# Gated attention beside an MLP on one core: a fourth up product early, PV output in two PSUM banks, x pieces on ScalarE's queue

## The chip, the core and the metric

The kernel runs on one of the eight cores of a Trainium2 chip. A core has five engines with an instruction stream each: TensorE (PE, matrix products into PSUM), VectorE (DVE), ScalarE (ACT), GpSimd (POOL) and SyncE (SP, which here only issues DMAs). The metric is the device time of one execution in microseconds (us), the median of several runs.

## The reference

All arrays are float32; x has 2048 rows of 640.

```python
xn = layernorm(x)                              # no scale, eps 1e-5
q = xn @ wq                                    # 32 heads of 128
k, v = the last 512 rows of the caches         # per head, no mask
p = softmax(q @ k.T * 128**-0.5)
s = (p @ v over all heads) @ wo                # 2048 x 640
h = relu(xn @ w1 + b1) ** 2                    # 640 -> 1728
g = silu(h @ w2 + b2)                          # 1728 -> 640
out = x + s * g
```

## The kernel before, in words

**Number format.** Every product is made of three float32r matmuls: each operand is split into a rounded high part and the remainder, and high x high, high x low and low x high are added in PSUM (`triple`, `products`). A "triple" of three 128x128x512 matmuls is the unit of PE's work; every split costs a copy (ACT) and a subtraction (DVE or POOL).

**Stages.** The 2048 rows are four tiles of 512 columns (the work is done transposed: features on partitions, rows along the free axis).

1. For tiles 0 to 2 the MLP: 14 chunks f of the hidden width, an up product (15 matmuls) and a down product (15 matmuls) each; the gate g goes to DRAM (`g_d`). Meanwhile the normalised x of each tile is written to DRAM in its two parts (`xT_d`).
2. Attention in 128 units: two halves of the rows, sixteen groups of two heads, two tiles, two heads. A unit has scores s (12 matmuls into four PSUM banks), the query product pq of two units later (15), the PV product o (12) and, for a pair of units, the output projection r (30).
3. The MLP of tile 3 (`late_*` functions): its up and down products (`lu`, `ly`) fill the last units and the tail after them, and the last gate, product with s and store end the kernel.

**A unit's softmax.** DVE folds each score bank to maxima (`max_fold`, tile rdm), ACT gathers 32-partition pieces (`gather`), DVE reduces them to a row (rowm); SP writes the row to DRAM (`m_d`) and loads it back spread over all partitions (`bm`), DVE subtracts it (`shift`, writes e and so frees the score banks), ACT takes the exponential (`expo`), ACT and POOL split it (`p_hi`, `p_lo`, tile pt). POOL adds the two halves (su), DVE folds the sum (`s_fold`, rds), ACT gathers, DVE inverts (sq, rows), SP writes and spreads it (`s_d`, `bs`), and DVE scales the PV output (`o_norm`), which ACT and DVE split (ot).

**Order.** From stage 2 on, the order is written out by hand: `at` and `on` put each step into `plan` with a due time, a unit's length being taken as PERIOD = 12.4 us, and at the end the steps are recorded in the order of these times. Every engine works strictly in its order, SP's queue too: a DMA that waits holds those behind it. The due times only sort; what an engine really waits for are semaphores.

**What the change touches.** `early_up`: three of tile 3's fourteen up products (chunks 11 to 13) are made during units 0 to 3, when there is no r and no early o to fill PE; their relu, square and split go to SBUF, and both parts to DRAM (`h_d`), from where `late_h` loads them in the tail. `q_mm` for unit 1 stands before unit 0. `load_xT` for the second half loads twenty pieces of 256 KB (two tiles, five column groups, two parts) on SP in units 59 to 64, in pairs at two places of a unit. `v_mm` writes every unit's o into one bank (tag "o"); r and pq use the banks "qr0" and "qr1"; `psx` is one more bank, used by early products and at the end. `finish` multiplies the first half's s by g and adds x in ten units of the second half.

In the tail, SP's order in unit 127 is: l1r3 (weights), five loads of x for the last gate (`late_x`, lx), then the unit's m_d and bm, later s_d and bs, and after these the weight loads l1r5 and l1r6. l1r6's buffer is free when POOL has split l1r4.

Of the kernel before, what the change touches and what calls it, by code (L numbers as in the profile page):

```python
# [8 lines left out]
F32 = mybir.dt.float32  # L9
# [11 lines left out]
def kernel(  # L21
# [65 lines left out]
    h_d = {f: dpool.tile([P, 2, NT], F32, name=f"h_d{f}") for f in range(FC - 3, FC)}  # L87

    def raw(ap):
        return ap.bitcast(F32)  # L90
# [19 lines left out]

    w1s, w2s = [], []
    for f, (f0, n) in enumerate(chunks):
        wp = wpa if f < FA else wpb
        if n < P:
            w1s.append([wp.tile([P, DC, 2 * n], F32R, name=f"w1s{f}")])
        else:
            if f < FA - 1:
# [312 lines left out]
    NQ = NT // B32  # L430
    NH = KC // 2

    EN = {"d": dve, "p": pool}

    XT, ACC, KT, VV, WQ, WO, Q, E, SC, MB, RD, PT, PO, OT, RB, QPS, FX, CL, PRS, RAW = (
        {} for _ in range(20)
    )
# [16 lines left out]
            for i in range(2)  # L454
        ]

    def load_xT(hf, t, i, cs):
        sp.dma_start(raw(XT[hf, t][i])[:, cs, :], xT_d[hf * TPH + t][i][:, cs, :])

    def raw_tile(kind, name):  # L460
        n = D if kind in "qo" else W
# [25 lines left out]
    def q_mm(i, cs):  # L487
        hf, g, t, h = units[i]
        if 0 in cs:
            QPS[i] = bank(f"pq{i}", int(i != 1))  # L490
# [150 lines left out]
    def load_finish(n, hf, t, d):  # L641
# [8 lines left out]
            }[n],  # L650
        )

    def finish(hf, t, d):
        fx, fg = (FX.pop((n, hf, t, d)) for n in "xg")
        a = ACC[hf, t][:, d, :] if hf else FX.pop(("s", hf, t, d))
        em, ea = "dp" if hf == 0 else "dd"
        EN[em].tensor_tensor(a, a, fg, op=ALU.mult)
        EN[ea].tensor_tensor(a, a, fx, op=ALU.add)
        store(sp, hf, t, d, a)

    def store(q, hf, t, d, a):
# [74 lines left out]
            c == DC - 1,  # L736
        )

    def early_split(f):
        r = LR.pop(f)  # L740
        hi, lo = (
            ap.tile([P, NT], F32R, tag=f"raw{n}", name=f"eh{f}_{n}", bufs=1) for n in "xg"
        )
        act.activation(hi, r, AF.Copy)
        dve.tensor_tensor(lo, r, raw(hi), op=ALU.subtract)
        for k, h in enumerate((hi, lo)):
            sp.dma_start(h_d[f][:, k, :], raw(h))

    def late_h(f):
        kind, bufs = ("wv", G) if f < FC - 1 else ("q", AHEAD + 1)  # L750
        LH[f] = pair(kind, [P, NT], f"lh{f}", bufs)
        for k in range(2):
            sp.dma_start(raw(LH[f][k]), h_d[f][:, k, :])

    def late_relu(f, kind):
        n = chunks[f][1]
        ph = LPH.pop(f)
# [9 lines left out]
    def late_square(f, eng=pool):  # L767
        eng.tensor_tensor(LR[f], LR[f], LR[f], op=ALU.mult)

    def late_split(f):  # L770
        n = chunks[f][1]
# [40 lines left out]
        store(sp, HALF - 1, TPH - 1, d, a)  # L812

    steps_n = len(steps)
    opened = (LATE - 1) * FC + FA
    for n in range(steps_n):
        mlp_step(n)
        if n == opened:
# [62 lines left out]
    for t in range(TPH):  # L881
        for c in range(DC):
            k, late = divmod(c + 1 - t, 2)
            w = (NG * UPG + t * G - 3 - AHEAD + t + k) * PERIOD + (8.5 if late else -1.6)
            if c == 0:
                at(w, open_xT, 1, t)
            for i in range(2):
                at(w + 0.7 * i, load_xT, 1, t, i, slice(c, c + 1))
    R_AT = (
        ((2 * PERIOD + 11.25, range(G)),),  # L890
        ((3 * PERIOD + 2.75, range(G)),),
# [9 lines left out]
    for i in range(NU):  # L901
        t0 = i * PERIOD

        def on(when, f, *a):
            at(t0 + when, f, *a)

        hf, g, t, h = units[i]
        for c in range(KC):
            on(0.68 * c, s_mm, i, c)
        if i + AHEAD < NU:  # L910
            q_at = 3.45 if i % G and i > UPG else 4.3
            for c in range(DC):
                on(q_at + 0.68 * c, q_mm, i + AHEAD, (c,))
            on(q_at + 3.5, q_hi, i + AHEAD)
            on(q_at + 4.1, q_lo, i + AHEAD)
# [12 lines left out]
        on(PERIOD + 6.2, s_fold, i)  # L928
        on(PERIOD + 8.0, gather, i, "s")
        on(PERIOD + 8.5, row, i, "s")  # L930
        on(18.6, p_lo, i, 1)
        for c in range(KC):
            on(PERIOD + 8.5 + 0.68 * c, v_mm, i, c)
        on(2 * PERIOD + 4.2, o_norm, i)
        on(2 * PERIOD + 4.9, o_hi, i)
        on(2 * PERIOD + 5.5, o_lo, i)
        if i % G == G - 1:
            for d in range(DC):
                last = i == NU - G - 1
# [19 lines left out]
    for item in order:  # L959
# [8 lines left out]
            at(now + 1.36, r_acc, NU - 1, n)  # L968
        else:
            for k, d in enumerate(range(DC)):  # L970
                for f in range(FC - 3, FC):
                    DOWN_AT.setdefault(f, now)
                    at(now + 0.68 * (3 * k + f - FC + 3), late_down, f, (d,))
                at(now + 2.04 * (k + 1), late_gate, d)
        now += STEP[kind]
    PREP = {
        0: z - 2 * PERIOD + 8.4,
# [31 lines left out]
    for f, u in sorted(DOWN_AT.items()):  # L1009
        free = DOWN_AT[f - 4] + STEP["d"] + 0.2 if f > 3 else 0.0  # L1010
        PREP2[f] = max(free, u - 7.0) if f else u - 5.0
        at(PREP2[f - 2] + 0.9 if f > 1 else u - 12.0, late_load, 2, f)
        at(PREP2[f], late_prep, 2, f)
        if f >= FA:
            at(now - 8.0 - 4.0 * (FC - f), late_h, f)
    EARLY_IN = (0,) * 7 + (1,) * 3 + (2,) * 3 + (3,) * 2
    for n, u in enumerate(EARLY_IN):
        k, c = divmod(n, DC)
        f = FA + k
        at(u * PERIOD + 8.0 + 0.01 * n, early_up, f, k % 2, c)  # L1020
        if c == DC - 1:
            at(u * PERIOD + 10.6, late_relu, f, "s")
            at(u * PERIOD + 12.0, late_square, f, dve)
            at((u + 1) * PERIOD + 7.6, early_split, f)
    at(z + 2.0, late_x)
    for d in range(DC):
        for n in "xg":
            at(z + 30.0 + 8.0 * d, load_finish, n, HALF - 1, 0, d)
        at(z + 36.0 + 8.0 * d, finish, HALF - 1, 0, d)
    for when, k, f, a in sorted(plan, key=lambda e: e[:2]):  # L1030
        f(*a)
# [46 lines left out]
```

## Time and profile before

| | |
|---|---|
| runs | 1979.72, 1978.24, 1979.13 us; median 1979.13 |
| profiled execution | 1978.84 us, its span 1977.1 us |
| mean granted TensorE clock | 0.999 |
| PE busy | 1952.0 us, 8576 matmuls |
| chain that ended last | PE 87%, DVE 5%, DMA 4%, ACT 2% |
| DMA | 220 MB, 111 GB/s over the span |

The profile is of one execution. In the timelines a row has the start in the span, the busy time, the engine, the operation, the tile written and the tiles read, the count, and in brackets the idle time before it with what ended it. Matmuls overlap: the busy time of a block is longer by a pipeline depth than its distance to the next block, so the pace is read from start to start. "SPq" rows are DMAs as SP issues them; their transfer comes after. L72 is the line of the helper through which the hand-ordered steps are recorded, so that groups are told apart by their tiles.

### The profile page before, as it was taken

How to read it: one execution, taken by the hardware profiler on the slowest of the kernel's cores; microseconds unless marked ns; L12 is line 12 of the kernel's file. 1: busy time of each engine (PE TensorE's matmuls, PEld its weight loads, DVE VectorE, ACT ScalarE, POOL GpSimd, SP SyncE). 2: the span in 40 equal slices, each digit the busy share in tenths (PEclk: the TensorE clock that was granted, in tenths of full speed). 3: DMA queues.
4: the chain of work that ended last, by engine and by line, in shares of the span. 5: the costliest groups of instructions: out<-in, count | busy, mean ns of one | idle time of the engine just before them, and what ended most of it. 6: DMA issues, size and time to landing. Idle time of an engine off the chain costs nothing.

```text
span 1977.1 us, 25595 instructions
## 1 busy us (share of the span) xinstructions
PE 1952.0 (99%) x8576; PEld 1607.7 (81%) x8576; DVE 1534.0 (78%) x2638; ACT 1186.0 (60%) x2035; POOL 1379.6 (70%) x763
## 2 busy tenths in 40 slices
PE   7999999999999999999999999999999999999998
PEld 6888887888888888888887788888888888888877
DVE  5533336788888888888888878888888888888864
ACT  4432326766666666666666676666666666666643
POOL 2121225888888888888887788888888888888841
PEclk9999999999999999999999999999999999999999
DMA  5431444333233333333335533333333333323454
GB/s 150 125 112 33 181 178 147 107 91 91 92 92 91 91 93 90 95 92 92 91 97 166 160 97 107 113 114 115 112 114 113 113 112 113 97 91 92 110 156 133
DMA packets 128917, 220.35 MB, mean 111 GB/s; under 512 B 23590, under 2 KB 38352, under 8 KB 127504
## 3 DMA queue, kind: packets, MB, share of 16 engines
q1 hardware_dynamic: 125792, 204.28, 34.3%
q0 software_dynamic: 2992, 14.43, 1.8%
q8 instruction: 67, 1.10, 0.2%
q14 instruction: 66, 0.54, 0.1%
HBM read 194.26 MB, written 24.39 MB: 111 GB/s over the span
## 4 chain that ended last, share of the span: by engine, by line
PE 87%; DVE 5%; DMA 4%; ACT 2%; issue 1%; POOL 0%; SPq 0%; DVEq 0%; ACTq 0%; POOLq 0%
PE r L72 20%; PE pq L72 20%; PE o L72 16%; PE s L72 16%; PE ph L95 2%; PE ph L97 2%; PE ph L96 2%; PE py L96 2%; PE py L95 2%; PE py L97 2%; PE ly L72 2%; PE lu L72 1%; DMA w1r<-in_w_dram 1%; DVE acc L72 1%; DMA bm<-m_d 1%
## 5 line engine op out<-in xcount | busy, mean ns | idle before, releaser
L72 POOL TENSOR_TENSOR pt<-e,pt 128x1024 fp32r<-128x1024 f32 x256 | 616.3, 2407 | 128.7 <-ACT pt L72 101.9
L72 PE MATMUL r<-ot,wo 128*128 128x512 f32 x1920 | 497.0, 389 | 0.3 <-DVE acc L72 0.3
L72 PE MATMUL pq<-ax,wq 128*128 128x512 f32 x1920 | 456.5, 389 | 0.8 <-DMA ax<-xT_d 0.6
L72 PEld LDWEIGHTS pq<-ax,wq 128*128 128x128 f32 x1920 | 360.4, 188 | 76.2 <-DMA ax<-xT_d 1.5
L72 PEld LDWEIGHTS r<-ot,wo 128*128 128x128 f32 x1920 | 360.3, 188 | 75.8 <-DVE acc L72 0.7
L72 PE MATMUL s<-q,wk 128*128 128x512 f32 x1536 | 369.6, 389 | 4.6 <-DVE e L72 4.6
L72 PE MATMUL o<-pt,wv 128*128 128x512 f32 x1536 | 371.1, 390 | 0.8 <-DVE ot L72 0.5
L72 ACT ACTIVATE e<-e 128x1024 f32<-128x1024 f32 x256 | 269.7, 1053 | 136.7 <-DVE e L72 116.7
L72 DVE TRANSPOSE_TENSOR_REDUCE rdm<-s 128x16 f32<-128x512 f32 x512 | 343.0, 707 | 3.0 <-PE s L72 2.9
L72 PEld LDWEIGHTS s<-q,wk 128*128 128x128 f32 x1536 | 288.0, 188 | 66.3 <-DVE e L72 6.0
L72 PEld LDWEIGHTS o<-pt,wv 128*128 128x128 f32 x1536 | 287.3, 188 | 64.5 <-DVE ot L72 2.9
L72 DVE TENSOR_TENSOR e<-s,bm 128x512 f32<-128x512 f32 x512 | 312.5, 666 | 18.4 <-DMA bm<-m_d 18.2
L72 POOL TENSOR_TENSOR su<-e,e 128x1024 f32<-128x1024 f32 x128 | 307.8, 2405 | 0.0
L72 ACT ACTIVATE pt<-e 128x1024 fp32r<-128x1024 f32 x256 | 271.8, 1062 | 7.8
L72 DVE TENSOR_TENSOR acc<-r,acc 128x512 f32<-128x512 f32 x300 | 203.0, 677 | 8.9 <-PE r L72 8.6
L289 POOL TENSOR_TENSOR r<-r 128x512 f32<-128x512 f32 (+1 forms) x42 | 43.8, 1044 | 216.3 <-ACT r L330 194.5
L72 ACT ACTIVATE ot<-o 128x512 fp32r<-128x512 f32 x128 | 76.7, 599 | 172.3 <-DVE o L72 172.3
L72 DVE TRANSPOSE_TENSOR_REDUCE rds<-su 128x32 f32<-128x1024 f32 x128 | 158.3, 1237 | 1.6 <-POOL su L72 1.6
L72 DVE TENSOR_TENSOR ot<-o,ot 128x512 fp32r<-128x512 f32 x128 | 88.5, 692 | 85.1 <-ACT ot L72 85.1
L72 ACT ACTIVATE q<-pq 128x512 fp32r<-128x512 f32 x128 | 76.6, 599 | 105.3 <-PE pq L72 105.3
L72 POOL TENSOR_TENSOR wq<-qr,wq 128x640 fp32r<-128x640 f32 x62 | 97.7, 1576 | 55.1 <-ACT wq L72 55.1
L72 POOL TENSOR_TENSOR wv<-vr,wv 128x512 fp32r<-128x512 f32 x64 | 83.0, 1297 | 73.6 <-ACT wv L72 66.5
(127 smaller groups left out, 2163.1 us busy)
## 6 DMA issues: line engine op xcount, KB each, us to landing
bm<-m_d SPq DMA_DIRECT2D x128, 256.0 KB, 3.3
bs<-s_d SPq DMA_DIRECT2D x128, 256.0 KB, 4.0
qr<-in_wq_dram SPq DMA_DIRECT2D x64, 320.0 KB, 4.3
or<-in_wo_dram SPq DMA_DIRECT2D x64, 320.0 KB, 3.8
kr<-in_kT_dram SPq DMA_DIRECT2D x64, 256.0 KB, 4.0
vr<-in_v_dram SPq DMA_DIRECT2D x64, 256.0 KB, 4.3
xT_d<-xT POOLq DMA_DIRECT2D x6, 1280.0 KB, 7.7
xb<-in_x_dram SPq DMA_DIRECT2D x16, 320.0 KB, 3.7
```

The lines of the kernel that those rows point to most:

```text
L72: ins = method(*args, **kwargs)
L95: nc.tensor.matmul(ps, ah, bh, start=first and i == 0, stop=False)
L96: nc.tensor.matmul(ps, ah, bl, start=False, stop=False)
L97: nc.tensor.matmul(ps, al, bh, start=False, stop=last and i == n - 1)
L289: nc.gpsimd.tensor_tensor(r, r, r, op=ALU.mult)
```

## The change

- A fourth up product of tile 3 (chunk 10) is made early: its 15 matmuls stand before unit 0, where unit 1's query product stood; that goes into unit 0, after its scores, and unit 2's query product to the end of unit 0. The four early products are spread as 5, 4, 4, 4 and 3 triples over the time before unit 0 and units 0 to 3.
- The early square no longer multiplies in SBUF: relu goes to SBUF, and one DVE instruction reads PSUM, adds the bias and multiplies by the relu. The result goes to DRAM whole, and the tail loads it (`late_h`, one step, four loads ahead of unit 127's m_d) and splits it there (`late_hs`).
- o of the even units from unit 4 on is written to the psx bank.
- The twenty x pieces of the second half are issued by ScalarE, four in each of units 59 to 63, behind the query's copy and ahead of the gather of the sums.
- The second p_hi of each unit stands behind the next unit's gather of maxima.
- The first half's product with the gate is a step of its own, half a unit earlier (`finish_gate`).
- In the tail, l1r5 and l1r6 are loaded ahead of unit 127's s_d and bs, and l2r1 ahead of l2r0; the last down products are in groups of four chunks rather than three.

```diff
-    FA = FC - 3
+    FO, FA = FC - 3, FC - 4
...
     def v_mm(i, c):
         hf, g, t, h = units[i]
         if c == 0:
-            PO[i] = pools["psb"].tile([P, NT], F32, tag="o", name=f"o{i}", bufs=1)
+            if i % 2 or i < UPG:
+                PO[i] = pools["psb"].tile([P, NT], F32, tag="o", name=f"o{i}", bufs=1)
+            else:
+                PO[i] = psx.tile([P, NT], F32, tag="x", name=f"o{i}")
...
+    def early_square(f):
+        r = LR[f]
+        dve.scalar_tensor_tensor(
+            r, LPH.pop(f), b1_sb[:, f : f + 1], r, op0=ALU.add, op1=ALU.mult
         )
+
+    def early_store(f):
+        sp.dma_start(h_d[f], LR.pop(f))
+
+    def late_h():
+        LR["h"] = pools["ep"].tile([P, DC, NT], F32, tag="x1", name="lh", bufs=TPH)
+        for f in range(FA, FC):
+            sp.dma_start(LR["h"][:, f - FA, :], h_d[f])
...
-    q_mm(1, range(DC))
-    q_hi(1)
-    q_lo(1)
+    EARLY_IN = (-1,) * 5 + (0,) * 4 + (1,) * 4 + (2,) * 4 + (3,) * 3
+    EARLY = [(FA + n // DC, n % DC) for n in range(len(EARLY_IN))]
+    for (f, c), u in zip(EARLY, EARLY_IN):
+        if u < 0:
+            early_up(f, 0, c)
...
+    for t, cols in enumerate(((2, 2, 1), (1, 2, 2))):
+        c = 0
+        for k, n in enumerate(cols):
+            w = (NG * UPG + t * G - 3 - AHEAD + k) * PERIOD + 7.9
             if c == 0:
                 at(w, open_xT, 1, t)
+            for _ in range(n):
+                for i in range(2):
+                    at(w + 0.01 * c, load_xT, 1, t, i, slice(c, c + 1), act)
+                c += 1
...
-        on(14.8, p_hi, i, 1)
+        on(PERIOD + 4.0, p_hi, i, 1)
...
+                    at(w + 2 * PERIOD + 6.0, finish_gate, 0, t, d)
...
-        5: z + PERIOD + 10.3,
-        6: z + PERIOD + 10.5,
+        5: z + PERIOD + 6.6,
+        6: z + PERIOD + 7.6,
...
+            at(z + 50.0 + 4.0 * (f - FA), late_hs, f)
+    at(z + 2.1, late_h)
```

More of the change, by code (lines that the diff above doesn't have):

```diff
@@ L86 @@
     s_d = [dpool.tile([P, DC, NT], F32, name=f"s_d{t}") for t in range(NTILE // 2)]
-    h_d = {f: dpool.tile([P, 2, NT], F32, name=f"h_d{f}") for f in range(FC - 3, FC)}
+    h_d = {f: dpool.tile([P, NT], F32, name=f"h_d{f}") for f in range(FC - 4, FC)}
     def raw(ap):
@@ L455, in open_xT, with load_xT @@
         ]
-    def load_xT(hf, t, i, cs):
-        sp.dma_start(raw(XT[hf, t][i])[:, cs, :], xT_d[hf * TPH + t][i][:, cs, :])
+    def load_xT(hf, t, i, cs, queue=sp):
+        queue.dma_start(raw(XT[hf, t][i])[:, cs, :], xT_d[hf * TPH + t][i][:, cs, :])
     def raw_tile(kind, name):
@@ L489, in q_mm @@
         if 0 in cs:
-            QPS[i] = bank(f"pq{i}", int(i != 1))
+            QPS[i] = bank(f"pq{i}", 1)
         ws, xs = WQ[hf, h], XT[hf, t]
@@ L651, in load_finish, with finish_gate @@
         )
+    def finish_gate(hf, t, d):
+        a = ACC[hf, t][:, d, :] if hf else FX["s", hf, t, d]
+        dve.tensor_tensor(a, a, FX.pop(("g", hf, t, d)), op=ALU.mult)
     def finish(hf, t, d):
-        fx, fg = (FX.pop((n, hf, t, d)) for n in "xg")
         a = ACC[hf, t][:, d, :] if hf else FX.pop(("s", hf, t, d))
-        em, ea = "dp" if hf == 0 else "dd"
-        EN[em].tensor_tensor(a, a, fg, op=ALU.mult)
-        EN[ea].tensor_tensor(a, a, fx, op=ALU.add)
+        (dve if hf else pool).tensor_tensor(a, a, FX.pop(("x", hf, t, d)), op=ALU.add)
         store(sp, hf, t, d, a)
@@ L737, in early_up, with late_hs @@
         )
[L739 to L742, printed above, removed]
-        )
+    def early_square(f):
+        r = LR[f]
+        dve.scalar_tensor_tensor(
+            r, LPH.pop(f), b1_sb[:, f : f + 1], r, op0=ALU.add, op1=ALU.mult
+        )
+    def early_store(f):
[4 more added lines that the diff above has]
+            sp.dma_start(LR["h"][:, f - FA, :], h_d[f])
+    def late_hs(f):
+        two = ap.tile([P, 2, NT], F32R, tag=f"pt{f % 2}", name=f"lh{f}", bufs=3)
+        hi, lo = LH[f] = [two[:, k, :] for k in range(2)]
+        r = LR["h"][:, f - FA, :]
         act.activation(hi, r, AF.Copy)
         dve.tensor_tensor(lo, r, raw(hi), op=ALU.subtract)
[L746 to L753, printed above, removed]
     def late_relu(f, kind):
         n = chunks[f][1]
-        ph = LPH.pop(f)
+        ph = LPH[f]
         r = LR[f] = raw_tile(kind, f"lr{f}")[:n, :]
@@ L765, in late_relu, with late_square @@
             act.activation(r, ph, AF.Relu, bias=bias)
[L767 to L768 removed]
+    def late_square(f):
+        pool.tensor_tensor(LR[f], LR[f], LR[f], op=ALU.mult)
     def late_split(f):
@@ L814 @@
     steps_n = len(steps)
-    opened = (LATE - 1) * FC + FA
+    opened = (LATE - 1) * FC + FO
     for n in range(steps_n):
@@ L909 @@
             on(0.68 * c, s_mm, i, c)
-        if i + AHEAD < NU:
-            q_at = 3.45 if i % G and i > UPG else 4.3
+        qs = [(i + AHEAD, 3.45 if i % G and i > UPG else 4.3, 4.1)]
+        if i == 0:
+            qs = [(1, 2.8, 4.1), (2, 9.1, PERIOD - 5.2)]
+        elif i < UPG:
+            qs = [(i + 2, 4.9 if i == 3 else 4.2, 4.1)]
+        for n, q_at, low in qs if i + AHEAD < NU else ():
             for c in range(DC):
-                on(q_at + 0.68 * c, q_mm, i + AHEAD, (c,))
-            on(q_at + 3.5, q_hi, i + AHEAD)
-            on(q_at + 4.1, q_lo, i + AHEAD)
+                on(q_at + 0.68 * c, q_mm, n, (c,))
+            on(q_at + 3.5, q_hi, n)
+            on(q_at + low, q_lo, n)
         for c in range(KC):
@@ L970 @@
             for k, d in enumerate(range(DC)):
-                for f in range(FC - 3, FC):
+                for f in range(FA, FC):
                     DOWN_AT.setdefault(f, now)
-                    at(now + 0.68 * (3 * k + f - FC + 3), late_down, f, (d,))
-                at(now + 2.04 * (k + 1), late_gate, d)
+                    at(now + 0.68 * ((FC - FA) * k + f - FA), late_down, f, (d,))
+                at(now + 0.68 * (FC - FA) * (k + 1), late_gate, d)
         now += STEP[kind]
@@ L1011 @@
         PREP2[f] = max(free, u - 7.0) if f else u - 5.0
-        at(PREP2[f - 2] + 0.9 if f > 1 else u - 12.0, late_load, 2, f)
+        at(PREP2[f - 2] + 0.9 if f > 1 else u - 12.0 if f == 0 else z + 11.0, late_load, 2, f)
         at(PREP2[f], late_prep, 2, f)
         if f >= FA:
[L1015 to L1020, printed above, removed]
+            at(z + 50.0 + 4.0 * (f - FA), late_hs, f)
+    at(z + 2.1, late_h)
+    for n, ((f, c), u) in enumerate(zip(EARLY, EARLY_IN)):
+        if u >= 0:
+            first = EARLY_IN[n - 2] < u or u == 3
+            at(
+                u * PERIOD + (6.3 if u == 0 else 3.4 if first else 8.2) + 0.01 * n,
+                early_up,
+                f,
+                (f - FA) % 2,
+                c,
+            )
         if c == DC - 1:
-            at(u * PERIOD + 10.6, late_relu, f, "s")
-            at(u * PERIOD + 12.0, late_square, f, dve)
-            at((u + 1) * PERIOD + 7.6, early_split, f)
+            done = u * PERIOD + (4.8 if u < 3 else 5.6) if u >= 0 else 0.3
+            at(done, late_relu, f, "s")
+            at(done + 0.6 if u >= 0 else 3.97, early_square, f)
+            at(max(u, 0) * PERIOD + 8.55, early_store, f)
     at(z + 2.0, late_x)
```

12 lines of the change are left out of this document (3 added, 9 removed).

## The prediction

> **What bounds the kernel.** I read the page first, then the busy time in six stretches, then the timelines of the stretches in which TensorE idles.
>
> ```profile
> PE 1952.0 (99%) x8576; PEld 1607.7 (81%) x8576; DVE 1534.0 (78%) x2638; ACT 1186.0 (60%) x2035; POOL 1379.6 (70%) x763
> ```
>
> ```profile
> 301.00:354.00 53.00, 49.88 (x214) 39.14 (x213) 39.35 (x66) 34.35 (x60) 36.45 (x27) 1.00 0.38 126
> 354.00:1050.00 696.00, 695.86 (x3069) 575.71 (x3068) 605.33 (x1042) 462.80 (x808) 565.90 (x284) 1.00 0.32 95
> 1050.00:1110.00 60.00, 57.06 (x246) 45.25 (x245) 47.38 (x85) 36.41 (x62) 43.90 (x23) 1.00 0.57 166
> 1110.00:1865.00 755.00, 755.00 (x3331) 624.82 (x3330) 656.21 (x1142) 501.35 (x876) 629.25 (x321) 1.00 0.36 109
> ```
>
> Behind the length of each stretch stands PE's busy time. TensorE is the bound: in the two long loops it idles 0.14 and 0.00 us, and one matmul takes 755.00 / 3331 = 0.2267 us. The change removes no matmul, so it can only move idle time, and that sits in three places: 3.12 us where attention starts, 2.94 us where the second half of the rows starts, and the tail, shown below.
>
> **Start of attention.** The PE timeline, blocks of scores only:
>
> ```profile
> 304.75 2.88 PE L72 MATMUL s<-q,wk 128*128 128x512 f32 x12
> ...
> 316.11 3.00 PE L72 MATMUL s<-q,wk 128*128 128x512 f32 x12 [0.32 <-DVE e L72]
> ...
> 328.80 3.01 PE L72 MATMUL s<-q,wk 128*128 128x512 f32 x12 [1.37 <-DVE e L72]
> ...
> 341.20 3.00 PE L72 MATMUL s<-q,wk 128*128 128x512 f32 x12 [0.99 <-DVE e L72]
> ...
> 353.93 1.30 PE L72 MATMUL s<-q,wk 128*128 128x512 f32 x5
> ```
>
> A unit's scores wait until the one before has its maximum subtracted (DVE writing e), because both use the same four banks. The built order has 48, 48, 48 and 51 matmuls between these five starts: 195 x 0.2267 = 44.2 us. The starts are 49.2 apart: 5.0 us are lost, restarts included. After the change the built order has 54, 51, 51 and 54 there, because unit 1's query product moves into unit 0; its 15 places before unit 0 go to the fourth up product, whose matmuls leave the tail. So PE reaches the four later starts after 12.24, 11.56, 11.56 and 12.24 us; measured were 11.36, 12.69, 12.40 and 12.73. The first then waits for nothing. For the middle two the chain has to shorten by 0.8 to 1.1, and part of it does:
>
> ```profile
> 317.68 0.68 DVE L72 TENSOR_TENSOR lr<-lr 128x512 f32<-128x512 f32 x1
> ```
>
> This square stands ahead of unit 1's four maximum folds; the new square, which reads PSUM, stands behind them and beside ScalarE's gather. The second copy of the exponentials (ACT pt) also goes behind the gather. Where both would have delayed the folds or the gather, 0.7 to 1 us goes. Against that, unit 3's query product now needs the bank that unit 2's query frees late: about 0.3 us. If nothing shortens, 12.69 - 11.56 + 12.40 - 11.56 = 2.0 us of waits stay, so the gain lies between 3.0 and 5.0. I take **-4.4**, nearer the upper end, since the square's row lies in the chain.
>
> **Second half's start.** PE, then SP's queue:
>
> ```profile
> 1052.37 2.88 PE L72 MATMUL s<-q,wk 128*128 128x512 f32 x12
> ...
> 1065.99 3.05 PE L72 MATMUL s<-q,wk 128*128 128x512 f32 x12 [1.18 <-DVE e L72]
> ...
> 1100.11 1.37 PE L72 MATMUL pq<-ax,wq 128*128 128x512 f32 x3 [0.65 <-DMA ax<-xT_d]
> ...
> 1106.10 2.88 PE L72 MATMUL s<-q,wk 128*128 128x512 f32 x12
> ```
>
> ```profile
> 1032.82 0.32 SPq L72 DMA_DIRECT2D m_d<-rowm  x1
> 1034.16 0.33 SPq L72 DMA_DIRECT2D bm<-m_d  x1
> ...
> 1054.71 0.42 SPq L72 DMA_DIRECT2D qr<-in_wq_dram  x1
> 1055.19 0.90 SPq L72 DMA_DIRECT2D ax<-xT_d  x2
> 1058.02 0.32 SPq L72 DMA_DIRECT2D m_d<-rowm  x1
> 1061.63 0.32 SPq L72 DMA_DIRECT2D bm<-m_d  x1
> ```
>
> Four units of 54 matmuls are 4 x 12.24 = 48.96 us; the starts from 1052.37 to 1106.10 are 53.73 apart, so 4.8 us are lost. The vector of maxima goes to DRAM (m_d) and comes back spread (bm). bm can be issued 1.34 us after m_d in an undisturbed unit (1032.82 to 1034.16), and 3.61 us where x pieces (ax) were issued just ahead on the same queue. The change issues the twenty ax pieces on ScalarE, four in each of five units, behind the query's copy. The last now go out a unit's second half before their use, so the wait of 0.65 goes.
>
> ScalarE pays for issuing them. No issue on its queue exists in this trace. The nearest are SP's (0.90 for two, 0.45 each) and POOL's:
>
> ```profile
> 302.12 2.94 POOL L377 DMA_DIRECT2D g_d<-sgl  x5 [8.96 <-PE py L97]
> ```
>
> These are 0.59 each. Behind the four issues on ScalarE stand the gather of the sums (rds), and through DVE's order the next unit's subtractions:
>
> ```profile
> 1048.78 0.72 ACT L72 ACTIVATE rds<-rds 32x32 f32<-32x32 f32 x3 [0.37 <-DVE rds L72]
> ...
> 1050.11 0.20 DVE L72 STREAM_TRANSPOSE rows<-sq 32x32 f32<-32x32 f32 x1
> ...
> 1051.16 2.48 DVE L72 TENSOR_TENSOR e<-s,bm 128x512 f32<-128x512 f32 x4 [0.85 <-DMA bm<-m_d]
> ...
> 1061.28 0.73 ACT L72 ACTIVATE rds<-rds 32x32 f32<-32x32 f32 x3 [1.31 <-DVE rds L72]
> ...
> 1062.90 0.20 DVE L72 STREAM_TRANSPOSE rows<-sq 32x32 f32<-32x32 f32 x1
> ```
>
> In the unit before 1052.37 the gather idles 0.37 and the rows end at 1050.31; with one subtraction (2.48 / 4 = 0.62) they leave 1.44 until the scores: a cover of 1.8 us. In the next unit PE would reach the scores at 1052.37 + 12.24 = 1064.61: 1.31 + (1064.61 - 1063.10 - 0.62 = 0.89) = 2.2. Four issues of 0.45 are 1.8: just covered. I leave 0.3 for that, and 0.3 for the maxima of the unit after, the last of the four, which still stand behind two weight loads and a store. **-4.2**; bounds -4.8, and -0.2 if an issue takes 0.74, as the slowest pair of SP here does (worked out with the last rival).
>
> **The loops.** The second bank for PV output takes at most their 0.14 us and its restart: **-0.2** (0 to -0.4). Moving the second exponential's copy behind the gather in all 128 units costs nothing: POOL takes it up only after its sum,
>
> ```profile
> L72 ACT ACTIVATE pt<-e 128x1024 fp32r<-128x1024 f32 x256 | 271.8, 1062 | 7.8
> ```
>
> ```profile
> 1232.34 0.79 ACT L72 ACTIVATE rdm<-rdm 32x64 f32<-32x64 f32 x3 [0.27 <-DVE rdm L72]
> 1232.52 2.40 POOL L72 TENSOR_TENSOR su<-e,e 128x1024 f32<-128x1024 f32 x1
> ```
>
> at 1234.92, and the copy would end at 1233.13 + 1.06 = 1234.19. Without these 0.7 us each lost 0.05 would be 6.4 us over 128 units. The ten gate products of the first half move ahead of the sum's fold (0.68 for such a row, lr above); the same 0.9 to 1.4 us before the scores hide them.
>
> **Tail.** Here the change adds work to SP's queue:
>
> ```profile
> 1866.41 2.41 SPq L72 DMA_DIRECT2D lx<-in_xT_dram  x5
> ...
> 1870.28 0.32 SPq L72 DMA_DIRECT2D m_d<-rowm  x1
> ...
> 1874.15 0.33 SPq L72 DMA_DIRECT2D bm<-m_d  x1
> ```
>
> ```profile
> 1883.24 2.55 PE L72 MATMUL lu<-ax,l1w 128*128 128x512 f32 x10 [0.72 <-ACT lr L72]
> ```
>
> The last unit's maxima already wait 3.87 instead of 1.34 us behind five loads of x: 0.51 for each. The changed order puts four more loads of the same size (the stored h) between those and m_d: 4 x 0.51 = 2.0 us. PE already waits at the end of this chain (bm, e, its exponential, then lr in ScalarE's order), so nothing covers it. In the built program each load also waits for the landing of the one eight places ahead, which holds m_d until the second lx is in. **+2.0**, between 0.4 (SP's issues alone: 1868.82 + 4 x 0.48 = 1870.7) and 2.6.
>
> Next the loads l1r5 and l1r6 move ahead of the last unit's sums (s_d, bs). l1r6 needs a buffer that POOL frees late:
>
> ```profile
> 1889.73 1.57 POOL L72 TENSOR_TENSOR l1w<-l1r,l1w 128x640 fp32r<-128x640 f32 x1
> ...
> 1890.66 0.32 SPq L72 DMA_DIRECT2D s_d<-rows  x1
> ...
> 1898.43 0.69 DVE L72 TENSOR_TENSOR ot<-o,ot 128x512 fp32r<-128x512 f32 x1 [0.66 <-ACT ot L72]
> ...
> 1899.67 2.88 PE L72 MATMUL r<-ot,wo 128*128 128x512 f32 x12
> 1902.87 4.42 PE L72 MATMUL r<-ot,wo 128*128 128x512 f32 x18 [0.32 <-DVE acc L72]
> ```
>
> s_d would go at 1889.73 + 1.57 + 0.45 = 1891.75 instead of 1890.66, +1.1, and behind a fresh load; one more load ahead costs 0.5 (above) to 2.3 (3.61 - 1.34). The end of ot has 1899.67 - 1899.12 = 0.55 us to spare: +1.0 to +2.8, or nothing if POOL slips less than PE. I take **+1.4** (0 to 2.8). The wait before 1902.87 goes, since l2r1 is loaded earlier: 1902.87 - 1899.67 - 2.72 = 0.48, **-0.5**. The four late splits (a copy and a subtraction each, 0.7 us by lr and ot above) lie beside a stretch in which PE has up and down products for tens of us; the fifteen matmuls gone from here were counted above.
>
> **Sum.** -4.4 - 4.2 - 0.2 + 2.0 + 1.4 - 0.5 = -5.9. The profiled execution took 1978.84 (span 1977.1); 1978.84 - 5.9 = 1972.9. The median of the runs shown is 0.3 higher, within their spread; I forecast **1973.0**.
>
> **Rivals.**
> - The tail stays hidden: the four loads drain in time, l1r6 too. For it: the queue's rows give no landing of lx itself; against: 3.87. It gives 1972.9 - 2.9 = 1970.0.
> - The pieces disturb the maxima from the other queue as well, because the bytes and not the order hold them: the 4.2 stay. For it: the engines are busier in that stretch than in any other quoted (0.57); against: m_d is two KB. It gives 1977.1. The Trainium skill, "DMA: Bandwidth & Descriptors", section "Issuing engines are not separate DMA queues", says that issuing from several engines only saves sequencer time, which is this rival; its section "Queues, rings and completion order" says that each engine takes turns between queue rows, which speaks for my term. No row here has two such queues loaded.
> - The early chain does not shorten: 2.0 of the 5.0 stay, 1974.3.
> - Slower: an issue on ScalarE costs more. Beyond 0.55 us each, two units lose 4t - 1.8 and three 4t - 2.2, together 20t - 10.2; less the 0.6 that I left, the sum is 1972.9 - 0.6 + 20t - 10.2. It passes 1978.84 at t = 0.84; at t = 1.05 it is 1983.1. For it: SP has 1.47 for two (0.74 each, 1976.9) in this stretch; against: 0.45 in most.
>
> ```profile
> 1068.07 1.47 SPq L72 DMA_DIRECT2D ax<-xT_d  x2
> ```
>
> **Chances.** My forecast 0.45, hidden tail 0.12, pieces still disturbing 0.15, early chain 0.18, slower 0.10 (half of it over 0.2%). About 0.2% (4 us, to 1975.2) is what a measurement of this kernel tells from no change. The early case with a dear tail, and the pieces' case, pass it; so faster 0.72, same 0.22, slower 0.06. Range 1969.4 (hidden tail, all of 5.0 gone) to 1978.3 (pieces and a tail dearer by 1.2); the likeliest alone 1971.2 to 1974.8.
>
> **What would show it.** Right: the five score starts 210 x 0.2267 + 0.6 = 48.2 us apart in sum, no wait for ax or bm near 1060 to 1110, bm in the last unit about 6 us behind m_d, a wait before the first late r. Wrong: scores waiting on e in the units with ScalarE's issues, each of those above 0.55 us, or any wait that repeats in the loops.

## The result, and the profile after

The changed kernel takes 1992.54 us (median of 6 runs, 1990.18 to 1994.10) against 1979.47 us for the kernel before in the same comparison: 1.0064 times, 95% interval 1.0054 to 1.0075. It is slower by 13 us; the prediction of 1973.0 us had the wrong sign. The profiled execution took 1992.3 us, its span 1990.5 us.

The busy line of the page after the change, to be held against the one of before:

```profile
PE 1960.8 (99%) x8576; PEld 1605.4 (81%) x8576; DVE 1548.8 (78%) x2639; ACT 1184.7 (60%) x2034; POOL 1377.2 (69%) x761
```

PE has the same 8576 matmuls, and its busy time hardly tells where 13 us went: it grew by 8.8 us although the work is the same, since the rows of disturbed blocks are longer (3.33 instead of 2.88 us for a PV block below). The number of matmuls in a stretch of fixed length is the better measure: at 0.2267 us each, 105 us hold 463 of them, 479 us hold 2113 and 90 us hold 397 (a matmul that lies across an end is counted too, so 2114 or 2115 can stand in a stretch without loss). What is missing, times 0.2267, is lost. Busy time by stretches, of before (columns: stretch, length, then busy time and count of PE, PEld, DVE, ACT, POOL, the granted PE clock, DMA share, GB/s):

```profile
1049.00:1154.00 105.00, 102.06 (x443) 82.33 (x442) 85.36 (x152) 66.91 (x119) 80.76 (x41) 1.00 0.51 153
1236.00:1715.00 479.00, 479.00 (x2114) 396.45 (x2113) 420.07 (x734) 314.66 (x548) 402.30 (x206) 1.00 0.36 113
1870.00:1960.00 90.00, 88.91 (x390) 72.20 (x389) 49.98 (x66) 36.77 (x58) 35.05 (x23) 1.00 0.52 159
```

And after the change:

```profile
301.00:354.00 53.00, 52.97 (x234) 43.53 (x233) 39.95 (x67) 34.63 (x61) 37.19 (x27) 1.00 0.38 123
354.00:1049.00 695.00, 695.00 (x3066) 575.00 (x3065) 601.82 (x1039) 460.88 (x805) 565.57 (x284) 1.00 0.32 95
1049.00:1154.00 105.00, 100.10 (x429) 79.24 (x428) 82.71 (x147) 64.71 (x115) 79.31 (x41) 1.00 0.47 149
1236.00:1715.00 479.00, 474.39 (x2055) 382.90 (x2054) 423.33 (x714) 305.88 (x532) 390.28 (x200) 1.00 0.37 110
1870.00:1960.00 90.00, 87.92 (x379) 71.01 (x378) 59.11 (x84) 41.98 (x71) 45.17 (x27) 0.98 0.51 152
```

Start of attention: 234 instead of 214, 4.5 us won. Second half's start: 429 instead of 443, 3.2 us lost. The loop of the second half, which had lost nothing: 2055 instead of 2114, 13.4 us lost. Tail: 379 instead of 390, 2.5 us lost. Together 14.6 us lost; the spans differ by 13.4, and most of the rest lies ahead of 301 us.

**Start of attention.** The first and the last of the five blocks of scores, PE's timeline after:

```profile
303.98 2.88 PE L72 MATMUL s<-q,wk 128*128 128x512 f32 x12
...
351.90 2.88 PE L72 MATMUL s<-q,wk 128*128 128x512 f32 x12
```

They are 47.92 us apart, with 210 matmuls (47.6 us) between them: 0.3 us are lost instead of 5.0.

**The second half's loop.** Ten units lose 1.2 to 1.8 us each; in them stand the ten gate products of `finish_gate`. One such unit, one of the two dearest, in rows of POOL, DVE and PE in the timeline after:

```profile
1487.45 2.39 POOL L72 TENSOR_TENSOR pt<-e,pt 128x1024 fp32r<-128x1024 f32 x1
...
1487.67 2.71 DVE L72 TENSOR_TENSOR fs<-fs,fg 128x512 f32<-128x512 f32 x1
...
1491.47 0.65 DVE L72 SCALAR_TENSOR_TENSOR q<-pq,q 128x512 fp32r<-128x512 f32 x1
...
1492.17 1.65 PE L72 MATMUL r<-ot,wo 128*128 128x512 f32 x6 [0.41 <-DVE q L72]
1494.03 3.04 PE L72 MATMUL s<-q,wk 128*128 128x512 f32 x12 [0.21 <-DVE e L72]
...
1502.35 3.33 PE L72 MATMUL o<-pt,wv 128*128 128x512 f32 x12
```

The product takes 2.71 us and ends at 1490.38, 0.54 us after POOL's subtraction (1489.84). Behind it DVE is 2 us late: with the query (PE's r waits 0.41 for its bank), with e (the scores wait 0.21), and the next PV block, 2.88 us long when nothing disturbs it, takes 3.33. In all ten units the product starts 0.2 to 0.7 us behind POOL's subtraction and ends 0.54 to 0.55 us behind its end. The groups of this product (behind the first bar busy time and mean ns, behind the second DVE's idle time before them), first after, then before:

```profile
L72 DVE TENSOR_TENSOR fs<-fs,fg 128x512 f32<-128x512 f32 x10 | 24.6, 2456 | 0.0
```

```profile
L72 DVE TENSOR_TENSOR fs<-fs,fg 128x512 f32<-128x512 f32 x10 | 7.2, 716 | 0.0
```

**Second half's start.** SP's queue, ScalarE's queue, DVE and PE after the change:

```profile
1058.33 0.33 ACTq L72 DMA_DIRECT2D ax<-xT_d  x1
...
1058.57 0.33 SPq L72 DMA_DIRECT2D bm<-m_d  x1
1058.69 1.41 ACTq L72 DMA_DIRECT2D ax<-xT_d  x3
...
1063.01 2.48 DVE L72 TENSOR_TENSOR e<-s,bm 128x512 f32<-128x512 f32 x4 [0.84 <-DMA bm<-m_d]
...
1075.09 0.32 SPq L72 DMA_DIRECT2D s_d<-rows  x1
1079.77 0.32 SPq L72 DMA_DIRECT2D bs<-s_d  x1
...
1090.69 3.05 PE L72 MATMUL s<-q,wk 128*128 128x512 f32 x12 [1.16 <-DVE e L72]
```

ScalarE issues four pieces in 1.74 us, as cheaply as assumed. But bm, issued in their midst, is there for DVE only 4.44 us later (1063.01 - 1058.57), and s_d holds bs for 4.68 us. No wait for x pieces is left, and in place of it the scores wait four times for e: at 1051.17 and 1090.69 us (1.02 and 1.16 us), while pieces go out, and at 1116.54 and 1143.10 us (0.74 and 1.38 us), where none does any more. The stretch therefore has to be read in two parts, with and without pieces, first before, then after:

```profile
1049.00:1110.00 61.00, 58.06 (x250) 46.10 (x249) 48.13 (x87) 37.36 (x65) 43.90 (x23) 1.00 0.57 166
1110.00:1154.00 44.00, 44.00 (x195) 36.23 (x194) 37.23 (x66) 29.55 (x55) 36.86 (x19) 1.00 0.43 135
```

```profile
1049.00:1110.00 61.00, 58.71 (x252) 46.24 (x251) 49.09 (x87) 37.76 (x65) 46.71 (x24) 1.00 0.53 170
1110.00:1154.00 44.00, 41.39 (x179) 33.00 (x178) 33.62 (x61) 26.95 (x50) 32.61 (x18) 1.00 0.38 119
```

44 us hold 194. Where the pieces are, the change holds about as many matmuls as before; the whole loss lies behind 1110 us.

**Tail.** SP, DVE and PE after:

```profile
1882.36 2.79 SPq L72 DMA_DIRECT2D lh<-h_d  x4
...
1885.25 0.43 SPq L72 DMA_DIRECT2D m_d<-rowm  x1
1891.25 0.33 SPq L72 DMA_DIRECT2D bm<-m_d  x1
...
1894.28 2.48 DVE L72 TENSOR_TENSOR e<-s,bm 128x512 f32<-128x512 f32 x4 [4.11 <-DMA bm<-m_d]
1896.68 0.68 DVE L72 TENSOR_TENSOR acc<-r,acc 128x512 f32<-128x512 f32 x1
1897.42 2.30 PE L72 MATMUL r<-ot,wo 128*128 128x512 f32 x6 [1.86 <-DVE acc L72]
```

bm follows m_d by 6.00 us, and PE waits 1.86 us ahead of the first late r for an addition that stands behind e in DVE's order.

### The profile page after: what moved, and what is told of

It is laid out like the page before. It is cut to its first block, busy times and chain, and to the rows that moved or that the text cites. A ratio compares the mean times of both kernels' runs of the same rounds, so it can differ in the third digit from the quotient of the medians.

```text
span 1990.5 us, 25577 instructions
## 1 busy us (share of the span) xinstructions
PE 1960.8 (99%) x8576; PEld 1605.4 (81%) x8576; DVE 1548.8 (78%) x2639; ACT 1184.7 (60%) x2034; POOL 1377.2 (69%) x761
## 5 line engine op out<-in xcount | busy, mean ns | idle before, releaser
L72 ACT ACTIVATE rdm<-rdm 32x64 f32<-32x64 f32 x384 | 97.8, 255 | 164.6 <-DVE rdm L72 161.4
L72 ACT ACTIVATE rds<-rds 32x32 f32<-32x32 f32 x384 | 89.7, 234 | 106.8 <-DVE rds L72 101.0
```

The source lines that it names most:

```text
L72: ins = method(*args, **kwargs)
```

## The experiments

All of the experiments have the late gate products except `gate_psum` and `gate_pool_lh_late_ax_sp`. The counts are matmuls in the three stretches, as above; the ratio is to the kernel before.

| kernel | median us | ratio, 95% interval | 1049-1154 (463) | 1236-1715 (2113) | 1870-1960 (397) |
|---|---|---|---|---|---|
| before | 1979.5 to 1980.3 | | 443 | 2114 | 390 |
| after | 1992.54 | 1.0064, 1.0054-1.0075 | 429 | 2055 | 379 |
| gate_back | 1979.48 | 1.0003, 0.9994-1.0013 | 430 | 2110 | 381 |
| gate_psum | 1978.51 | 0.9994, 0.9984-1.0003 | 437 | 2115 | 380 |
| gate_back_ax_sp | 1978.32 | 0.9994, 0.9984-1.0003 | 440 | 2110 | 378 |
| gate_back_lh_late | 1976.04 | 0.9986, 0.9976-0.9995 | 432 | 2111 | 394 |
| gate_pool_lh_late_ax_sp | 1977.98 | 0.9992, 0.9983-1.0001 | 436 | 2094 | 393 |
| gate_back_ax_act_pairs | 1979.33 | 0.9999, 0.9990-1.0009 | 448 | 2110 | 374 |
| gate_back_lh_l1_late | 1975.40 | 0.9979, 0.9970-0.9988 | 429 | 2107 | 398 |
| gate_back_loops_back | 1979.10 | 1.0003, 0.9993-1.0012 | 428 | 2113 | 382 |
| mended_ax_sp | 1974.73 | 0.9973, 0.9962-0.9983 | 434 | 2109 | 398 |
| mended_ax_act | 1975.43 | 0.9976, 0.9967-0.9984 | 433 | 2109 | 395 |
| mended_ax_act_behind | 1975.32 | 0.9977, 0.9967-0.9987 | 431 | 2111 | 398 |
| mended_ax_sp_one_bank | 1973.12 | 0.9965, 0.9951-0.9979 | 436 | 2113 | 398 |

### Late gate products again

```diff
-                    at(w + 2 * PERIOD + 6.0, finish_gate, 0, t, d)
+                    at(w + 3 * PERIOD - 0.7, finish_gate, 0, t, d)
```

> The ten gate products fs*fg of the first half's tiles stand again directly ahead of their additions, one unit's half later; all else as in the changed kernel. Theory A (the product, placed where GpSimd runs its second p_lo, is held until that ends and takes 2.4 us instead of 0.7): the ten units with stalls of 0.1 to 0.6 us ahead of r, s and o lose them, the product takes 0.7 us, about 11 us go, 1981 us. Theory B (the loops lose by the second output bank or the moved p_hi): the stalls stay and the time is 1990 to 1993 us.

Measured: 1979.48 us, 13.1 us less than the change, and 2110 matmuls in the second half's loop. Theory A holds, a little beyond its size; B falls. One stall remains, 0.65 us ahead of o at 1643.7 us.

### The same product with one operand from PSUM

```diff
-        dve.tensor_tensor(a, a, FX.pop(("g", hf, t, d)), op=ALU.mult)
+        g = FX.pop(("g", hf, t, d))
+        dve.tensor_tensor(a, a, g if hf else LASTO[0], op=ALU.mult)
```

> The ten gate products stay where the change put them, but multiply by the unit's output bank, which lies in PSUM, instead of the loaded gate (so the first half's results are multiplied by something else than the gate). One operand in SBUF, one in PSUM, same place, same VectorE order, same loads. Theory A (two operands in SBUF beside GpSimd's work): the product takes 0.7 us beside the running p_lo and 9 to 11 us go, 1981 to 1984 us. Theory C (VectorE has no room for any operation at that place): the product's place alone costs the time and it stays within 3 us of 1992.5.

Rows of POOL and DVE in this run's timeline, at the place shown above for the change:

```profile
1283.15 2.42 POOL L72 TENSOR_TENSOR pt<-e,pt 128x1024 fp32r<-128x1024 f32 x1
...
1283.73 0.68 DVE L72 TENSOR_TENSOR fs<-fs,o 128x512 f32<-128x512 f32 x1
```

```profile
L72 DVE TENSOR_TENSOR fs<-fs,o 128x512 f32<-128x512 f32 x10 | 6.8, 677 | 0.0
```

Beside the same POOL instruction the product now takes 0.68 us, and the loop has 2115 matmuls: no loss at all. The place was good; what cost 13 us is that both operands came from SBUF while POOL worked there. Theory C falls. The gate's load is issued as before but no longer read, so by itself this run doesn't exclude a late load. The change's trace does: DVE's idle time before its ten products is 0.0 us (the group's row above), and their ends follow POOL's. What a wait for this load looks like stands in the run with the product on GpSimd below.

### x pieces on SyncE's queue

```diff
-                    at(w + 0.01 * c, load_xT, 1, t, i, slice(c, c + 1), act)
+                at(w + 0.7 * i, load_xT, 1, t, i, slice(c, c + 1))
```

(with the old places of the pairs)

> As gate_back, and the second half's x pieces are issued on SyncE's queue in the old pattern of two pieces each half unit. Theory A (four pieces at a time from the scalar engine's queue slow the row maxima and the inverse sums more than two at a time on SyncE's own queue hold them up): the losses from 1049 to 1154 us fall from 8.4 to about 4.8 us, so 3.6 us less than gate_back, about 1977.5 us. The prediction's term, were it right: 4.2 us more than gate_back, 1985 us. Neither: within 1 us of gate_back.

Measured: 1978.32 us, 1.2 us less, with overlapping intervals; 440 matmuls against 430, 2.3 us. The direction is theory A's, the size two thirds of it by the count and a third by the time; but the count is of one profile each, and in the other profiles with the change's bursts it lies between 428 and 437, so the difference is not clear of the spread. The prediction's term, by which this run should have been 4.2 us slower, falls.

### Stored rows loaded later

```diff
-    at(z + 2.1, late_h)
+    at(z + 26.0, late_h)
```

> As gate_back, and the four loads of the stored rows for the last tile are issued 24 us later, behind the last unit's inverse sums. Theory A (they hold SyncE and share the engines with m_d127, so the last scores' shift and the addition behind it come late): m_d127 takes 2 us instead of 6, the wait of 1.9 us ahead of r and the slower matmuls behind it go, 3 to 3.5 us less than gate_back, about 1977.7 us. Rival: the loads now collide with the weight loads of the last tile, and less than 1 us is won.

SP's queue and the tail's stretch in this run:

```profile
1873.60 0.32 SPq L72 DMA_DIRECT2D m_d<-rowm  x1
1876.39 0.33 SPq L72 DMA_DIRECT2D bm<-m_d  x1
```

```profile
1870.00:1960.00 90.00, 89.77 (x394) 73.04 (x393) 54.73 (x75) 40.33 (x65) 35.98 (x22) 1.00 0.52 155
```

bm follows m_d by 2.79 us instead of 6.00, the tail holds 13 matmuls more, and the median falls by 3.4 us. Theory A holds.

### Three mends, the product on GpSimd

The edits of the last two, and:

```diff
-        dve.tensor_tensor(a, a, FX.pop(("g", hf, t, d)), op=ALU.mult)
+        (dve if hf else pool).tensor_tensor(a, a, FX.pop(("g", hf, t, d)), op=ALU.mult)
```

> Three mends at once: the ten gate products at the change's early place, but on GpSimd, behind the p_lo that blocked VectorE; the four loads of the stored rows 24 us later; the x pieces on SyncE's queue in the old pattern. From the sums of the losses so far: 1979.5 less 1.1 (the stall at 1642 us that is left with the late gate) less 2.9 (tail) less 2.2 (second half's start): 1973.3 us, 1972 to 1974.5. Rival: the product's 1.3 us on GpSimd push its weight splits and p_lo back, and stalls of 0.3 us or more a unit come back: 1976 us or more.

```profile
1283.69 1.30 POOL L72 TENSOR_TENSOR fs<-fs,fg 128x512 f32<-128x512 f32 x1 [0.60 <-DMA fg<-g_d]
1284.94 2.40 POOL L72 TENSOR_TENSOR pt<-e,pt 128x1024 fp32r<-128x1024 f32 x1
```

POOL took the product ahead of its p_lo, not behind it as the expectation had it, and in two of the ten units waited for the gate's load on top (0.60 us in the one shown). PE then waits for pt in ten units (2094 matmuls, 4.3 us lost). The rival holds: 1977.98 us. The run also shows that a wait for the load stands as idle time before the product, not in its length, and it bounds the wait: here the product starts 3.00 us after the start of POOL's sum (1280.69), and in the changed kernel VectorE's product starts 2.93 us after it (1286.55, the sum at 1283.62). A late load could account for about 0.1 us of the 1.7 by which that product was too long, not for the rest.

### Pairs on the scalar engine's queue

```diff
+            w = (NG * UPG + t * G - 3 - AHEAD + t + k) * PERIOD + (8.5 if late else -1.6)
...
-                    at(w + 0.01 * c, load_xT, 1, t, i, slice(c, c + 1), act)
+                at(w + 0.7 * i, load_xT, 1, t, i, slice(c, c + 1), act)
```

> As gate_back, with the x pieces still on the scalar engine's queue, but two at a time in the old pattern of places instead of two to four at one place. Theory A (the number issued at once is what slows the row maxima): the losses from 1045 to 1160 us fall to the 5.2 us of the run with SyncE's queue, about 1978 us. Theory B (the other queue as such lets the pieces run beside the small transfers, which on SyncE stand ahead of them in order): the losses stay at 7.5 us or more, 1979.5 us or more.

The run did not do what it was made for: ScalarE has little between the two places of a unit, and issues four pieces in a row again, only 1.1 to 2.6 us later against bm. SP, ScalarE's queue and DVE:

```profile
1057.90 0.34 SPq L72 DMA_DIRECT2D bm<-m_d  x1
...
1059.70 0.33 ACTq L72 DMA_DIRECT2D ax<-xT_d  x1
...
1061.44 2.43 DVE L72 TENSOR_TENSOR e<-s,bm 128x512 f32<-128x512 f32 x4
```

With the first piece 1.4 us or more behind it, bm is ready for DVE after 3.3 to 3.8 us, in five units; in the changed kernel, with the first piece between 0.9 us ahead of it and 0.7 us behind, it took 4.4 to 4.7 in four units (in the fifth DVE was busy until 4.1). The stretch holds 448 matmuls, the most of all versions. The time does not follow, since this profile's tail is the worst of all (374), so the run settles neither theory.

### Last tile's weight loads back

```diff
-        5: z + PERIOD + 6.6,
-        6: z + PERIOD + 7.6,
+        5: z + PERIOD + 10.3,
+        6: z + PERIOD + 10.5,
```

> As gate_back_lh_late, and the last tile's weight loads l1r5 and l1r6 again at their old places, behind the last unit's inverse sums. The prediction's term (those loads ahead of s_d127 cost 1.4 us): 1.4 us less, 1974.6 us. Rival (they hold up nothing, and their early place takes a wait of the last tile's up product away): 0.5 to 1.5 us more, 1976.5 to 1977.5 us.

Measured: 1975.40 us, 0.6 us less with overlapping intervals, and 398 matmuls in the tail instead of 394, none lost. By the trace the prediction's direction is right, its 1.4 us about twice what there is; the rival's wait of an up product doesn't appear.

### The loops' other edits undone

```diff
-        on(PERIOD + 4.0, p_hi, i, 1)
+        on(14.8, p_hi, i, 1)
...
-            if i % 2 or i < UPG:
+            if True:
```

> As gate_back, with the loops' other two edits undone: one output bank for all units, and p_hi of the second half of the keys at its old place. The prediction's term (0.2 us for both): 1979.7 us, and the small stalls of the first half's loop come back with some 0.4 us. Theory B (they are worth more, by waits for the output bank in many units): 1981 us or more. Theory C (the moved p_hi causes the stalls of 0.2 us ahead of o at the second half's start and the one at 1642 us): 1977 to 1978 us.

Measured: 1979.10 us against 1979.48. Theory B falls. No stall comes back in the first half's loop, and the one at 1643.7 us is gone (2113); but PV products wait four times for the one bank between 1070 and 1130 us, 0.2 to 0.45 us each.

### All mends, on either queue

```diff
-                    at(w + 2 * PERIOD + 6.0, finish_gate, 0, t, d)
+                    at(w + 3 * PERIOD - 0.7, finish_gate, 0, t, d)
-        on(PERIOD + 4.0, p_hi, i, 1)
+        on(14.8, p_hi, i, 1)
-    at(z + 2.1, late_h)
+    at(z + 26.0, late_h)
-        5: z + PERIOD + 6.6,
-        6: z + PERIOD + 7.6,
+        5: z + PERIOD + 10.3,
+        6: z + PERIOD + 10.5,
```

and the pairs of x pieces as in the runs above, on SyncE's queue in the first run and on ScalarE's in the second.

> All that the runs so far showed to cost time is undone: late gate products, the stored rows and l1r5, l1r6 behind the last unit's inverse sums, p_hi at its old place, the x pieces in pairs on SyncE's queue. What is left of the change is the early up product with its squares and the second output bank. From gate_back_lh_l1_late (1975.4 us, losses 8.4 us at the second half's start and 1.7 us in the second half): less 3 us and less 1.4 us, 1971 us; 1970.5 to 1973 us. Rival (the prologue's own spread and the small losses take it back, or the early chain's 4 us are paid for elsewhere): 1975 us or more.

> The same with the pairs on the scalar engine's queue. If the queue is worth something by itself (its single profile showed 3.8 us of losses at the second half's start against 5.2 and 6.1 us with SyncE's): 1 to 2 us less than on SyncE's queue, 1969.5 us. If the queue makes no difference: the same within 0.7 us.

Measured: 1974.73 and 1975.43 us. Both are faster than before by a quarter of a per cent, and the two make no difference that can be told; as in the run with pairs above, ScalarE issued four pieces in a row here (1048.04 to 1049.36 us), so pairs on its queue are tested by no run. The first expectation missed by 3.7 us. Its gains on the two stretches did not come in full: the second half's start holds 434, and the stall at 1643 us stands there again (2109) although p_hi is back.

### The burst behind the gather

The same mends, with the change's own bursts, and:

```diff
-            w = (NG * UPG + t * G - 3 - AHEAD + k) * PERIOD + 7.9
+            w = (NG * UPG + t * G - 3 - AHEAD + k) * PERIOD + 9.0
```

> As mended_ax_act, but with the change's own bursts of two to four pieces on the scalar engine's queue, behind the gather of the sums and the weight copies instead of ahead of them. Theory A (a burst delays the spread maxima only if it is issued within about 1 us of them, whatever the queue; in five profiles bm took 4.1 to 5.1 us then, and 3.2 to 3.8 us where the pieces came 1.4 us or more behind): bm takes 3.2 to 3.8 us in all units from 1030 to 1090 us, the losses there are 4 to 5.5 us instead of 7.7, and the time is 1972 to 1974 us. Theory B (four pieces at once delay the small transfers wherever they stand): bm or the sums' row take over 4 us in most of these units and the losses stay at 7.5 us or more, 1975 us or more.

```profile
1060.34 0.33 SPq L72 DMA_DIRECT2D bm<-m_d  x1
...
1062.12 0.33 ACTq L72 DMA_DIRECT2D ax<-xT_d  x1
...
1063.96 0.32 SPq L72 DMA_DIRECT2D s_d<-rows  x1
1067.50 0.32 SPq L72 DMA_DIRECT2D bs<-s_d  x1
```

bm is quick in four of five units (3.3 to 3.5 us), and in the one where the burst fell 0.1 us behind it it took 4.7: so far theory A. But s_d, now just behind the burst, holds bs for 3.5 to 5.7 us, where pairs on SyncE's queue left it 1.3 to 3.4; the stretch holds 431, and the time is unchanged. So four pieces at once delay whichever small transfer stands next to them. Of theory B's signs the time came (1975.32 us); bm or bs over 4 us came in two of the five units only, and of the 7.3 us that the stretch loses 2.5 lie behind 1110 us, where no piece goes out.

### One output bank

As mended_ax_sp, and:

```diff
-            if i % 2 or i < UPG:
+            if True:
```

> As mended_ax_sp, with one output bank for all units. If the stall of 1.0 us at 1642 us (in every profile with late gate products and two output banks, 0.95 to 1.7 us with the small ones, and 0.3 us with one bank) comes with the second bank: it goes, and 0.7 to 1 us with it, 1973.9 us. If the second bank is worth the prediction's 0.2 us: 1974.9 us and small stalls of 0.1 to 0.5 us from 354 to 1045 us. If the stall depends on neither: it stays at 1.0 us.

Measured: 1973.12 us and 2113 matmuls; the stall at 1643 us is gone, and none comes back in the first half's loop (3068 from 354 to 1049 us). So the stall needs the second bank; it needs the late gate products too, since gate_psum has both banks and no stall. This is the fastest version, 0.9965 times the kernel before (0.9951 to 0.9979). Its interval overlaps that of two banks, so that the second bank costs time is likely, not shown.

## Why the prediction was wrong

**The failed step: the gate products.** The prediction wrote that the ten gate products "move ahead of the sum's fold (0.68 for such a row, lr above); the same 0.9 to 1.4 us before the scores hide them". They cost 13.1 us, all of the loss. The cover was there for that price: with an operand from PSUM the product at that place took 0.68 us and cost nothing. The price was wrong: 2.46 us in the mean, because POOL starts its subtraction just ahead. Being 1.6 to 2.0 us late, DVE then holds up not the scores alone but also r, which waits for the bank that the query frees, and the next PV block, which waits for pt; the prediction had named no cover for these two. A row that shows the dear price stands in the trace of before, POOL and DVE in the tail:

```profile
1881.19 2.39 POOL L72 TENSOR_TENSOR pt<-e,pt 128x1024 fp32r<-128x1024 f32 x1 [5.04 <-ACT pt L72]
1881.61 2.52 DVE L72 TENSOR_TENSOR lh<-lr,lh 128x512 fp32r<-128x512 f32 x1 [0.95 <-ACT lh L72]
```

A subtraction of the same size as the product, both operands in SBUF, takes 2.52 us and ends 0.55 us after POOL's (1884.13 against 1883.58). Of the eleven subtractions of this group the median took 0.69 us, this longest one 2.52: such an instruction has two prices, and I took the row of an undisturbed one (of the three squares in that row's own group the other two took 0.90). The Trainium skill states the rule, in "SBUF — State Buffer", sections "Who interferes with whom" and "SBUF: two separate sides": a VectorE instruction with two inputs in SBUF contends with a GpSimd instruction that reads SBUF, and the one that starts later waits for the whole of the other. These rows agree: 2.46 us with two inputs in SBUF, 0.68 with one. With the price of 2.52 the step would have been costed at ten times about 1.8 us of DVE's order, and "any wait that repeats in the loops", which the prediction had only as a sign of being wrong, would have been a rival.

Without this step the change would still have missed: gate_back takes 1979.48 us, as much as before, and the forecast was 1973.0. Most of the rest is the second half's start.

**Start of attention: right.** -4.4 forecast, 4.5 won, in the size and the place; the 0.3 us that stay are the wait for unit 2's query bank. The rival of an early chain that doesn't shorten falls. The prediction gave two reasons for the shortening, the square and the second copy of the exponentials: with that copy at its old place (gate_back_loops_back) the stretch from 301 to 354 us still holds 234, so the copy was not needed; the square was not tested alone.

**Second half's start: wrong.** -4.2 forecast; nothing was won, and 3.2 us were lost besides. The two have to be told apart. ScalarE's issues cost 0.33 to 0.46 us each, the cover for them sufficed, and the slower rival (0.84 an issue) falls. What failed where the pieces are is the assumption that maxima on SyncE's queue go undisturbed when the pieces are on another. They don't: m_d lets bm go after 1.35 us in some units, but bm then takes 4.4 to 4.7 instead of 3.4 to 3.6 us, and s_d up to 4.7 instead of 3.1 at most, so that from 1049 to 1110 us 252 matmuls stand against 250. That is my second rival, to which I gave 15 in 100: "the 4.2 stay". Its rule in the Trainium skill, "DMA: Bandwidth & Descriptors", section "Issuing engines are not separate DMA queues", is what the runs bear out: pairs on SyncE's queue were no slower than bursts on ScalarE's (1978.32 against 1979.48 us; 1974.73 against 1975.43 and 1975.32), and up to 1110 us the bursts hold 249 to 260, SyncE's pairs 254 to 257.

The 3.2 us of the count lie behind 1110 us, where the results of the first half are being stored. There the kernel before lost nothing (195), and all thirteen versions hold 179 to 186, with bursts or pairs, on either queue, with one bank or two. SP issues the same transfers in the same order, but m_d lands later behind a store of results; SP's queue, first before, then after:

```profile
1111.89 0.66 SPq L72 DMA_DIRECT2D m_d<-rowm  x1
1113.86 0.32 SPq L72 DMA_DIRECT2D bm<-m_d  x1
```

```profile
1108.65 0.32 SPq L72 DMA_DIRECT2D m_d<-rowm  x1
1112.45 0.32 SPq L72 DMA_DIRECT2D bm<-m_d  x1
```

That is 3.80 us instead of 1.97. No run undoes it and the prediction has no term for it. What moved there stays open; for the kernel before there is one profile.

**Loops, the other edits: too small to test.** 0.2 us were forecast for the bank and nothing for p_hi; undoing both changed 0.4 us, within the spread. With the late gate products the second bank brings a stall of 0.6 to 0.8 us instead, so for it even the sign is in doubt.

**Tail: right in mechanism, too small.** The four loads cost +2.0 by the sum, 3.4 us by the run without them. The wait ahead of the first late r came as foretold, 1.86 us in the changed kernel; the rest there is PE's clock behind it (last section). In gate_back, from which the 3.4 are measured, the clock stayed at 1.00, and two waits of 1.42 and 0.87 us with their slow restarts stand in its place. The loads l1r5 and l1r6 were put at +1.4: they cost about 0.6 us once the tail was otherwise clear, and nothing in the changed kernel, where r of unit 127 starts at 1916.73 without a wait. The -0.5 for l2r1 came in the changed kernel (the largest gap there is 0.14 us), but in gate_back and gate_back_lh_late 0.4 to 0.5 us stood there again.

The sum of the terms with their measured sizes, -4.5 + 3.2 + 13.4 + 2.5 = 14.6, stands for what happened. Without the products and the bursts no gain can be told (1978.32 us, interval up to 1.0003); with all mends there is one, 5 to 7 us.

## What to carry to other kernels

Before an elementwise step on VectorE is moved, look at what GpSimd does at the new place: with both inputs in SBUF it pays up to the rest of GpSimd's instruction, and with one input in PSUM it doesn't. When one row or a group's median is used as a price, look at the group's longest member and what ran beside it. Large transfers moved to another engine's queue still delayed the small ones next to them in time here; keep them off the round trips that gate TensorE. And split a stretch before explaining its loss: part of this one had no x piece in it, and that part held the loss.

## What the runs showed that was not expected

After the wait of 1.86 us in the tail TensorE's granted clock fell; the stretch of 4.6 us behind the start of that r shows 0.63 in the mean:

```profile
1897.40:1902.00 4.60, 4.36 (x12) 2.78 (x13) 3.69 (x3) 3.34 (x5) 4.12 (x2) 0.63 0.61 217
```

12 matmuls stand where 20 would: 1.8 us (0.22 of it a further wait), as much as the wait itself. In gate_back waits of 1.42 and 0.87 us within 5 us at the same place left the clock at 1.00, and so did one of 1.78 us in gate_psum, so the length alone does not decide; in the run with the pairs on ScalarE's queue a wait of 2.85 us was followed by the same slow pace of 0.43 us a matmul. So the wait of 1.86 us cost TensorE about twice its length, which no row of the kernel before showed; what decides stays open.
